# Layer B's normalized rows transposed by DMA instead of on TensorE

## The chip, the cores and the metric

One Trainium2 chip, one core. The metric is the device time of one execution of the whole program in microseconds, as the median of several runs. The time before is 1449.24 us (three runs, 1447.66 to 1451.28).

## The reference

Four layers, A B A B, on x of 2048 rows by 512 (f32). Both kinds use 32 heads of 16. Layers 0 and 2 share the weights of A, layers 1 and 3 those of B.

```
x = x + A(layernorm(x));  x = x + B(layernorm(x));  x = x + A(layernorm(x));  x = x + B(layernorm(x))

layernorm(x) = (x - mean) / sqrt(var + 1e-5)            # over the 512 of a row
A: q, k, v = x @ wqkv;  each row attends to 8 rows: itself and those 2, 4, ... 14 before it;  softmax;  @ wo
B: q, k, v = x @ wqkv;  each row attends to the 256 rows up to itself;  softmax;  @ wo
```

## The kernel before

**Chunks.** Rows are worked in 8 chunks of 256 (C), each as two halves of 128 rows. `layer_a(l, c)` and `layer_b(l, c)` describe one layer of one chunk. The calls are issued for layers 0 and 1, chunk by chunk (A0, B0, A1, B1, ... A7, B7), then for layers 2 and 3 (A8, B8 ... A15, B15). Here "chunk n of B" is B0 to B15. Layer B of a chunk needs layer A's output of the same chunk, and the keys and values of the chunk before it.

**Matrix products in two f16 parts.** A projection takes its rows as a high part xh (f16) and a low part xl (what the rounding left, f16), and the weights likewise: three f16 matmuls stand for one in f32 (lines 1015 to 1017 for the transposed outputs, 1035 to 1038 for the others). TensorE contracts over partitions, so xh and xl are needed transposed: features on partitions, rows along the free axis.

**The norm** (`norm`, line 923) is shared by both layers. Per half: statistics on VectorE (936, 939), then scale and shift for both halves (942 on VectorE, 945 on GpSimd, 948 on VectorE). Then it goes one of two ways, by the condition at line 957:

- Layer A, except the first chunk of layer 0: ScalarE writes the normalized half xn in f32 (964) and copies it to f16, ht (974); the rest xn - ht is computed in place on GpSimd or VectorE (970); two DMA transposes issued by SyncE move ht to xh (976) and the rest to xl (977).
- Layer B, and that first chunk: ScalarE writes xn (986), TensorE transposes its four 128 x 128 blocks in f32 into a PSUM bank (990), ScalarE casts the bank to xh (995), VectorE subtracts to get xl (996).

xn and ht have two buffers each, shared by all chunks; xh and xl have two of each.

**After the norm.** `proj_t` (1000) computes a projection in 16 steps of three matmuls for each 256 x 512 result; each step reads the whole of xh and xl, both halves. Layer B does that for keys and queries; the results are split in two f16 parts again (1270, 1273), written to DRAM (1283, "puts") and read back into a stacked layout (1294). Values and the output projection use `proj_n` (1030), 8 steps for each half. In `layer_b` a score step is one small group of four matmuls: first for the row maxima (1336, 1339, with VectorE's 1358 and 1354 behind it), then again for the exponentials (1430, 1432, then ScalarE's 1436 and GpSimd's mask 1445). The maxima reach the second group by way of DRAM (1391, 1397). A value step is 16 matmuls (1462). `finish` (1049) splits the attention's output (1059, 1061), projects it and adds it to x (1069); the sum is y, stored to DRAM (1080).

**The order.** Nothing is issued where it is written. Each step is a task for one engine's queue, added by `plan.add`; `ORDER` (line 40), a table written out in the file, gives each task its place in the queue of its engine, one list for each chunk of each layer. A negative place also moves the task to the other engine that it names (`alt`): the rests (970, 1061, 1203), the products of layer A (1152), the sums (1247 to 1251), the scaling of B's output (1537) and the scaled row maxima (1378, 1380). An engine takes its queue strictly in order. Steps of several chunks are interleaved in it: while a chunk of B is normalized, TensorE works on score and value steps and on the output projection of the B chunks before it.

```
if layers[l] == "A" and (l, c) != (0, 0):
    plan.add("ACT", 0.71, xnorm, r=[xs[t][1], vrs], w=[vxn])
    plan.add("ACT", 0.48, lambda xn=xn, ht=ht: nc.scalar.copy(ht.t, xn.t), r=[vxn], w=[vht])
    plan.add("POOL", 1.12, rest, r=[vxn, vht], w=[vlt], mode="S", alt=("DVE", 0.6))
    plan.add("SP", 1.24, ... nc.sync.dma_start_transpose(xh.t[:, :, sl], ht.t), r=[vht], w=[vh], size=16)
    plan.add("SP", 1.24, ... nc.sync.dma_start_transpose(xl.t[:, :, sl], low()), r=[vlt], w=[vl], size=16)
```

Of the kernel before, what the change touches and what calls it, by code (L numbers as in the profile page):

```python
# [19 lines left out]
S = 2048  # L20
# [5 lines left out]
W = 8  # L26
# [14 lines left out]
    "S": [4, 9, 6, 3],  # L41
    "pA": [3, -7, 2, 0, 8, 19, 10, 26, 15, 6, 18, 8, 21, 5, 3, 6, 4, 12, 27, 16, 33, 19, 30, 10, 25, 9, 24, 13, -30,
        10, 13, 8, 12, 11, 11, 33, 64, 39, 74, 42, 22, 46, 25, 51, 45, 26, 57, 27, 52],
    "pB": [14, 18, 15, 31, 17, 21, 22, 30, 24, 29, 26, 32, 19, 28, 27, -59, 59, 112, 66, 131, 68, 41, 100, 44, 84,
        71, 42, 96, 45, 89, 49, 99, 39, 88, 70, 51, 101, 43, 87, 24, 38, 51, 1, 29, 30, 28, 31],
    "W": [43, 0, 38, 89, 22, 20, 11, 1, 37, 12, 31, 39, 17, 2, 3, 14, 25, 41, 40, 23, 8, 66, 28, 58, 5, 84, 42, 13,
        35, 6, 7, 30, 15, 82, 9, 34, 24, 4, 16, 103, 92, 32, 36, 18, 10, 44, 85, 101, 88, 192, 116, 115, 86, 187,
        196, 189, 139, 90, 195, 193, 197, 100, 194, 87, 91, 165, 134, 190, 432, 448, 3387, 3365, 3254, 3451, 3389,
        3367, 3421, 3393, 3369, 3376, 3460, 3426, 3455, 3454, 3435, 3424, 3445, 3534, 3540, 3531, 3471, 3441, 3542,
        3536, 3543, 3527, 3539, 3533, 3526, 3535, 3541, 3537, 3440, 3459, 3437, 3448, 3461, 3446, 3538, 3532],  # L50
    "A0": [1, 0, 0, 2, 1, 3, 4, 5, 5, 1, 21, 5, 14, 2, 29, 7, 20, 0, 2, 45, 46, 47, 48, 49, 50, 51, 52, 67, 68, 69,
        71, 75, 76, 79, 81, 14, 24, 53, 54, 55, 56, 57, 59, 60, 61, 62, 63, 65, 70, 72, 77, 78, 80, 17, 23, 95, 97,
        98, 99, 105, 110, 113, 120, 94, 96, 102, 107, 108, 109, 118, 124, 36, 37, 12, 14, 37, 36, 38, 35, 73, 41, 44,
        40, 43, 83, 47, 48, 49, 50, 93, 54, 55, 53, 56, 104, 33, 11, 60, 61, 34, 62, 63, 64, 35, 65, 129, 67, 15, 73,
        17, 130, 69, 16, 72, -75, 136, 75, 18, 79, -81, 141, 76, -79, 77, 20, 46, 19, 166, 167, 168, 169, 170, 171,
        173, 175, 25, 83, 54, 50, -83, 178, 179, 180, 181, 182, 183, 184, 185, 18, 86, 84],
    "B0": [85, 91, 90, 92, 93, 22, 94, 53, 198, 55, 97, 54, 199, 56, 98, 200, 202, 206, 210, 212, 213, 214, 215, 201,
        203, 204, 205, 207, 208, 209, 211, 63, 105, 62, 104, 33, 35, 37, 36, 34, 32, 46, 45, 49, 53, 216, 217, 219,
        220, 222, 224, 227, 228, 218, 221, 223, 225, 226, 229, 230, 231, 65, 108, 64, 107, 41, 43, 40, 39, 44, 42,
        47, 48, 50, 52, 233, 235, 236, 238, 239, 244, 247, 248, 66, 234, 237, 240, 242, 243, 245, 249, 250, 67, 257,  # L60
        129, 253, 118, 258, 128, 252, 119, 251, 117, 255, 123, 254, 120, 259, 127, 130, 70, 132, 55, 56, 267, 71,
        273, 74, 42, 296, 271, 73, 275, 75, 43, 298, 78, 264, 136, 276, 150, 270, 144, 278, 151, 268, 141, 265, 145,
        272, 146, 261, 140, 153, 77, 155, 64, 65, 311, 84, 309, 83, 45, 378, 343, 87, 342, 88, 46, 387, 98, 305, 166,
        304, 167, 260, 131, 279, 149, 314, 171, 302, 165, 287, 164, 297, 162, 172, -174, 174, 66, 67, 388, 99, 368,
        94, 50, 436, 364, 93, 385, 97, 51, 438, 111, 285, 156, 319, 175, 365, 184, 360, 182, 320, 177, 359, 183, 313,
        170, 321, 176, 186, -189, 190, 87, 92, 412, 103, 406, 100, 52, 421, 418, 106, 424, 107, 56, 431, 109, 98, 95,
        99, 100, 251, 102, 103, 269, 270, 124, 71, 486, 487, 488, 489, 490, 491, 493, 495, 108, 284, 112, 125, 72,
        492, 496, 498, 499, 500, 501, 502, 503, 109, 285, 120],
    "A1": [12, 4, 22, 27, 7, 9, 28, 8, 31, 15, 16, -35, 16, 21, 19, 20, 10, 20, 23, 13, 21, 106, 111, 119, 121, 126,
        133, 135, 137, 138, 142, 150, 151, 152, 154, 155, 159, 40, 48, 114, 117, 122, 123, 125, 127, 128, 132, 147,  # L70
        157, 158, 160, 161, 162, 163, 164, 38, 47, 144, 146, 148, 153, 156, 172, 174, 191, 140, 143, 145, 149, 176,
        177, 186, 188, 52, 60, 23, 31, 106, -26, 81, 95, 232, 111, 109, -28, 110, 241, 113, 115, 112, 114, 246, 116,
        -30, -29, -31, 256, 121, 122, 68, 124, 125, 126, 69, -34, 262, 137, 36, 133, 34, 263, 135, 35, 134, -139,
        266, 139, 37, 142, 39, 269, 143, 40, 147, -149, 72, 38, 274, 277, 280, 281, 282, 283, 284, 286, 59, 152, 91,
        76, 41, 288, 289, 290, 291, 292, 293, 294, 295, 60, 158, 83],
    "B1": [154, 157, 159, 160, 161, 44, 163, 79, 306, 81, 169, 80, 307, 82, 168, 315, 316, 317, 318, 322, 323, 324,
        325, 326, 327, 329, 330, 331, 332, 333, 335, 85, 178, 86, 179, 72, 68, 73, 71, 69, 70, 80, 85, 86, 88, 328,
        334, 336, 341, 345, 347, 348, 349, 337, 338, 340, 344, 351, 352, 353, 354, 89, 180, 90, 181, 78, 79, 74, 75,
        77, 76, 81, 82, 90, 94, 399, 401, 410, 414, 419, 422, 423, 425, 108, 429, 430, 433, 434, 440, 441, 442, 445,
        112, 420, 223, 226, 394, 203, 209, 402, 208, 210, 389, 201, 202, 384, 195, 196, 407, 214, 216, 417, 219, 221,  # L80
        427, 229, 230, 232, 110, 234, 96, 97, 459, 119, 460, 118, 65, 469, 451, 115, 452, 116, 68, 481, 457, 117,
        447, 113, 67, 482, 466, 122, 470, 123, 69, 483, 126, 428, 231, 236, 454, 252, 254, 444, 241, 243, 435, 235,
        238, 449, 247, 249, 450, 248, 250, 443, 242, 245, 453, 255, 257, 259, 121, 265, 104, 106, 514, 137, 515, 139,
        75, 542, 506, 135, 513, 140, 76, 543, 546, 145, 529, 142, 77, 585, 540, 143, 552, 147, 78, 593, 156, 473,
        267, 268, 505, 287, 289, 504, 286, 288, 485, 276, 281, 467, 261, 263, 464, 258, 260, 484, 278, 279, 472, 266,
        274, 290, 136, 293, 113, 117, 572, 150, 573, 151, 79, 604, 595, 158, 592, 155, 82, 614, 596, 157, 616, 162,
        86, 626, 606, 159, 612, 160, 85, 627, 168, 528, 296, 298, 547, 301, 302, 560, 305, 307, 583, 315, 317, 582,
        314, 316, 571, 310, 312, 541, 299, 300, 561, 306, 308, 318, 153, 323, 136, 138, 624, 165, 625, 166, 89, 652,
        635, 170, 630, 169, 90, 655, 637, 171, 650, 174, 93, 662, 649, 175, 654, 176, 95, 664, 179, 142, 141, 148,
        149, 373, 150, 151, -106, -108, 189, 106, 702, 703, 704, 705, 706, 707, 708, 709, 116, 401, 182, 191, 109,  # L90
        710, 712, 714, 715, 716, 717, 718, 719, 157, 407, 162],
    "A2": [7, 9, 11, 13, 17, 23, 26, 7, 32, 59, 61, -104, 63, 58, 57, 58, -103, 62, 61, 26, 32, 339, 346, 350, 355,
        356, 357, 361, 362, 367, 369, 371, 372, 373, 374, 379, 383, 92, 95, 299, 300, 301, 303, 308, 310, 312, 358,
        363, 366, 370, 375, 376, 380, 381, 382, 91, 96, 390, 391, 393, 398, 400, 405, 408, 409, 392, 396, 397, 403,
        411, 413, 415, 416, 101, 104, 48, 53, -48, 187, 189, 185, 377, 192, 191, 194, 193, 386, 199, 197, 200, 198,
        395, 205, 207, 204, 206, 404, 211, 213, 102, 217, 218, 220, 105, -55, 426, 228, 57, 233, 58, 437, 239, 60,
        237, 59, 446, 246, 64, 244, 61, 439, 240, 63, 253, -257, 114, 62, 455, 456, 458, 461, 462, 463, 465, 468, 57,
        262, 105, 120, 66, 471, 474, 475, 476, 477, 478, 479, 480, 101, 271, 107],
    "B2": [264, 272, 273, 275, 277, 73, 280, 127, 494, 129, 282, 128, 497, 130, 283, 508, 509, 510, 512, 516, 517,
        518, 519, 507, 511, 520, 521, 523, 524, 526, 527, 138, 295, 141, 297, 125, 122, 118, 119, 123, 124, 132, 133,  # L100
        140, 146, 525, 531, 534, 538, 544, 545, 548, 549, 522, 530, 532, 533, 535, 536, 537, 539, 146, 304, 144, 303,
        129, 130, 127, 131, 128, 126, 135, 134, 139, 144, 631, 632, 633, 634, 638, 639, 642, 643, 172, 644, 646, 647,
        648, 651, 653, 658, 659, 177, 640, 350, 352, 613, 335, 336, 617, 339, 340, 602, 329, 331, 603, 328, 330, 629,
# [1510 lines left out]
```

## Time and profile before

| what | value |
|---|---|
| median of three runs | 1449.24 us |
| the profiled execution | 1449.52 us |
| its span, first to last instruction | 1447.8 us |
| mean granted TensorE clock | 0.961 |
| DMA traffic | 130.45 MB, mean 90 GB/s |
| transposes on TensorE (L990) | 136 |
| DMA transposes (L976, L977) | 30 and 30 |

In the lines of the profile PE is TensorE, PEld its weight loads, DVE is VectorE, ACT ScalarE, POOL GpSimd, SP SyncE; SPq is SyncE's queue, where DMAs are issued. L990 is line 990. A row of a timeline has the start in us, the length in us, the engine, the line, the operation and how many of them, and in brackets the idle time before it with what ended that. A row of a group has the busy time in us, the mean in ns, then the idle time of the engine just before and what ended it. A row of waits has who waited for whom: us in total, how often, the longest.

### The profile page before, as it was taken

Reading aid. Unit: us, or ns where it says so; the run is one execution under the profiler, and the core shown is the slowest. Engines: PE = TensorE matmul, PEld = TensorE weight load, DVE = VectorE, ACT = ScalarE, POOL = GpSimd, SP = SyncE. Lnnn points to the kernel's source line nnn. Section 1 sums busy time; section 2 is a strip of 40 time slices with the busy share of each in tenths; the row PEclk is TensorE's granted clock in tenths of the full one; section 3 lists DMA queues with packets and bytes.
Section 4 is the critical chain, followed back from the end, with each engine's and each line's share of the span. In section 5 each row is a group of like instructions: output and inputs, shape, how many; then the busy total and the mean of one; then the engine's idle time right before and its main releaser. Section 6 shows DMA issues by size and latency. Waiting matters only on the chain.

```text
span 1447.8 us, 35225 instructions
## 1 busy us (share of the span) xinstructions
PE 1343.2 (93%) x13918; PEld 780.3 (54%) x13918; DVE 1166.8 (81%) x2263; ACT 732.8 (51%) x1049; POOL 687.1 (47%) x780
## 2 busy tenths in 40 slices
PE   9985989999899999999999898999989999999997
PEld 7651636546364564746556363644637465474654
DVE  6867697896979879797996969698696977969694
ACT  6621335554565455555554444455454545445564
POOL 2415264472835427273471717355382743727233
PEclk9995989999999999999999999999999999999999
DMA  7232233225242333423233343323423143233232
GB/s 241 66 79 75 74 78 112 72 82 125 48 125 77 84 89 88 108 63 112 59 83 111 73 119 76 121 61 86 112 60 117 49 110 87 72 105 76 67 102 61
DMA packets 135944, 130.45 MB, mean 90 GB/s; under 512 B 68449, under 2 KB 94561, under 8 KB 135777
## 3 DMA queue, kind: packets, MB, share of 16 engines
q1 hardware_dynamic: 135520, 127.93, 32.6%
q8 instruction: 109, 1.79, 0.5%
q14 instruction: 59, 0.48, 0.1%
q10 hardware_dynamic: 256, 0.26, 0.1%
HBM read 67.11 MB, written 43.48 MB: 76 GB/s over the span
## 4 chain that ended last, share of the span: by engine, by line
PE 48%; DVE 21%; POOL 7%; issue 7%; DMA 6%; SPq 5%; ACT 5%; DVEq 0%; POOLq 0%; ACTq 0%
PE banks L1015 8%; PE banks L1016 7%; PE banks L1017 7%; PE banks L1462 5%; DVE m L1354 4%; PE banks L1160 3%; PE banks L1430 3%; DVE banks L1358 3%; ACT p L1436 3%; DVE pw L1242 3%; PE banks L1037 3%; PE banks L1035 3%; PE banks L1336 2%; POOL pw L1249 2%; PE banks L1038 2%
## 5 line engine op out<-in xcount | busy, mean ns | idle before, releaser
L1436 ACT ACTIVATE p<-banks,sclB 128x768 f32<-128x768 f32 x480 | 418.2, 900 | 282.4 <-PE banks L1432 203.9
L1445 POOL TENSOR_SCALAR_AFFINE_SELECT p<-p 128x1024 f32<-128x1024 f32 x240 | 263.5, 1106 | 345.0 <-ACT p L1436 300.7
L1354 DVE TENSOR_REDUCE m<-banks 128x2 f32<-128x512 f32 x448 | 296.9, 683 | 3.6
L1358 DVE COPY_PREDICATED banks<-maskt,banks 128x256 f32<-128x256 int16 x448 | 179.4, 420 | 65.0 <-PE banks L1339 55.5
L1462 PE MATMUL banks<-p,v 128*32 128x128 f32 (+1 forms) x3840 | 196.2, 332 | 5.7 <-POOL p L1445 4.4
L1152 DVE TENSOR_TENSOR pr<-kv,q 128x512 f32<-128x512 f32 x231 | 156.6, 727 | 31.6 <-PE banks L1160 17.5
L1462 PEld LDWEIGHTS banks<-p,v 128*32 128x32 f32 x3840 | 106.4, 110 | 97.6 <-issue 36.1
L1430 PE MATMUL banks<-stk,stk 64*128 64x256 f16 x960 | 133.7, 283 | 24.0 <-DVE m L1354 7.9
L1242 DVE TENSOR_TENSOR pw<-banks,kv 128x1024 f32<-128x1024 f32 x128 | 152.7, 1212 | 3.7 <-PE banks L1229 2.2
L1339 PE MATMUL banks<-stk,stk 48*128 48x128 f16 (+1 forms) x1024 | 128.5, 252 | 18.0 <-DVE m L1350 9.2
L1249 POOL TENSOR_TENSOR pw<-pw 128x512 f32<-128x512 f32 x100 | 127.3, 1273 | 13.5 <-DVE pw L1242 11.4
L1336 PE MATMUL banks<-stk,stk 48*128 48x128 f16 (+1 forms) x896 | 112.7, 253 | 20.1 <-DVE m L1354 9.2
L1430 PEld LDWEIGHTS <-stk 64*128 64x128 f16 x960 | 55.2, 94 | 119.4 <-issue 111.7
L1273 DVE SCALAR_TENSOR_TENSOR el<-banks,eh 128x512 f16<-128x512 f32 x64 | 42.6, 685 | 89.8 <-DMA re<-eh 45.2
L1432 PE MATMUL banks<-stk,stk 64*128 64x128 f16 x960 | 107.6, 222 | 0.0
L1336 PEld LDWEIGHTS <-stk 48*128 48x128 f16 x896 | 51.2, 94 | 100.3 <-issue 90.0
L1250 POOL TENSOR_TENSOR pw<-pw 128x256 f32<-128x256 f32 x100 | 73.0, 730 | 7.8
L1015 PE MATMUL banks<-xh,wB1h 128*128 128x256 f16 x256 | 71.0, 277 | 1.6 <-ACT p L1436 0.7
L1016 PE MATMUL banks<-xl,wA0h 128*128 128x256 f16 x256 | 70.1, 274 | 2.3 <-DMA xl<-xn 2.3
L1339 PEld LDWEIGHTS <-stk 48*128 48x128 f16 x1024 | 53.1, 96 | 34.6 <-issue 29.1
L1015 PE MATMUL banks<-xh,wA0h 128*128 128x256 f16 x256 | 70.4, 275 | 1.4 <-DMA xh<-ht 1.0
L1160 PE MATMUL banks<-pr,sel 128*32 128x512 f32 x512 | 71.0, 609 | 0.5 <-DVE pr L1152 0.3
(197 smaller groups left out, 3052.6 us busy)
## 6 DMA issues: line engine op xcount, KB each, us to landing
stk<-re SPq DMA_DIRECT2D x256, 96.0 KB
re<-eh SPq DMA_DIRECT2D x128, 128.0 KB
re<-el SPq DMA_DIRECT2D x64, 128.0 KB
xm<-y SPq DMA_DIRECT2D x32, 256.0 KB
y<-xm SPq DMA_DIRECT2D x32, 256.0 KB
oc<-os SPq DMA_DIRECT2D x120, 64.0 KB
os<-scr SPq DMA_DIRECT2D x15, 512.0 KB
x<-in_A_x_dram SPq DMA_DIRECT2D x16, 256.0 KB
```

Of the source, the lines that this page charges most:

```text
L1015: nc.tensor.matmul(ps[mp].t[:, i], wh, xh, start=k == 0, stop=False)
L1016: nc.tensor.matmul(ps[mp].t[:, i], wh, xl, start=False, stop=False)
L1152: E.tensor_mul(pr.t, window(kv[1].t, m, 64 * tq, 64)[:, 0], qb)
L1242: nc.vector.tensor_mul(pw.t, pb.t.unsqueeze(1).broadcast_to([P, 2, W, 64]), v)
L1336: nc.tensor.matmul(ps.t[:, par, 0 : (2 - qb) * P], lhs, stk[hf, bef][r, col, qb * P :], start=True, stop=True)
L1339: nc.tensor.matmul(ps.t[:, par, (2 - qb) * P : 3 * P], lhs, stk[hf, now][r, col, : (1 + qb) * P], start=True, stop=True)
L1354: nc.vector.tensor_reduce(out=m.t[:, :, u, qb], in_=ps.t[:, :, 0 : 2 * P], op=ALU.max, axis=AX.X)
L1358: nc.vector.copy_predicated(t[:, :, 0:P], maskt[:, 0:P].bitcast(I16).unsqueeze(1).broadcast_to([P, 2, P]), t[:, :, 2 * P : 3 * P])
L1430: nc.tensor.matmul(o[:, two], k[:, jf * P : (jf + 1) * P], q, start=True, stop=True)
L1436: nc.scalar.activation(pt.t[:, :, 2 * i : 2 * i + 2].rearrange("p s m q -> p m s q"), ps.t[:, :, : 3 * P].rearrange("p m (s q) -> p m s q" ...
L1445: nc.gpsimd.affine_select(out=v, in_=v, pattern=[[0, 8], [-1 if b == 0 else 1, P]], compare_op=ALU.is_gt if b == 0 else ALU.is_ge, fill=0. ...
L1462: nc.tensor.matmul(o, v[:, jj, 17 * h : 17 * h + 32], rhs, start=z == 0 and (b == 0 or first), stop=z == 1 and b == 1, tile_position=(0, 3 ...
```

## The change

One condition in `norm` is different. Layer A's chunks are treated as before; all of layer B's chunks take the way by DMA, too, except the first chunk of layer 1.

```diff
         for t in range(2):
-            if layers[l] == "A" and (l, c) != (0, 0):
+            if c or l > 1:
                 xn = buf("pxn", [P, D], F32, "xn", f"xn{l}_{c}_{t}")
                 ht = buf("pxn", [P, D], F16, "ht", f"ht{l}_{c}_{t}")
```

So in 15 chunks of B the transposes on TensorE (990), the casts (995) and the subtractions (996) are gone, and copies (974), rests (970) and DMA transposes (976, 977) take their place: per half one copy, one rest and two DMA transposes. A chunk of B has two tasks more. `ORDER` is another table throughout, with places for the new tasks and other places for the old ones; it also names other engines for some of them:

| tasks on their second engine | before | after |
|---|---|---|
| B's rests (970) on VectorE | - | 5 of 30 |
| A's rests (970) on VectorE | 13 of 30 | 13 of 30 |
| products (1152) on GpSimd | 25 of 256 | 32 of 256 |
| rests of e (1203) on GpSimd | 8 of 16 | 7 of 16 |
| sums (1247) on VectorE | 28 of 128 | 28 of 128 |
| scaled maxima (1380) on VectorE | 20 of 64 | 16 of 64 |
| scaling of B's output (1537) on GpSimd | 13 of 30 | 19 of 30 |
| rests of B's output (1061) on VectorE | 7 of 32 | 3 of 32 |

840 rows, old and new, of the table ORDER are left out of this document.

## The prediction

> **What bounds the kernel now.** I read the page first: its span, the busy times and the chain that ended last.
>
> ```profile
> span 1447.8 us, 35225 instructions
> PE 1343.2 (93%) x13918; PEld 780.3 (54%) x13918; DVE 1166.8 (81%) x2263; ACT 732.8 (51%) x1049; POOL 687.1 (47%) x780
> ...
> PE 48%; DVE 21%; POOL 7%; issue 7%; DMA 6%; SPq 5%; ACT 5%; DVEq 0%; POOLq 0%; ACTq 0%
> ```
>
> The profiled execution took 1449.5 us (1.7 around the span), the median of the three runs is 1449.24: one number for my purpose, and the sum is made against 1449.5. PE is busy for 93% of the span and is almost half of the chain; DVE at 81% is next. A busy PE can still be one that waits behind pipelined ends, so I looked at single stages and at PE's waits.
>
> ```profile
> 486.00:570.00 84.00, 80.42 (x881) 46.63 (x879) 70.29 (x124) 42.49 (x60) 39.34 (x44) 0.98 0.32 86
> ```
>
> ```profile
> PE banks L990 <- ACT xn L986: 10.2, 10, 3.5
> PE banks L1336 <- DVE m L1354: 9.2, 19, 2.1
> ```
>
> The columns of the stretch are us, then PE, PEld, DVE, ACT and POOL busy with counts, clock, DMA share, GB/s. In this stretch of 84 us, about one A chunk and one B chunk, PE idles only 3.6 us at a granted clock of 0.98, while DVE leaves 14 us and POOL over 40. So in the middle of the kernel **time is PE's own work plus the few waits that PE's order can't cover**. The largest of these waits belongs to the operation that the change removes: the transposes of line 990 wait 10.2 us for xn.
>
> **The PE side of the change.** 15 of B's 16 chunks change, two halves each: 30 halves, 120 transposes of the 136 (the rest is chunk 0 of layers 0 and 1).
>
> ```profile
> L990 PE MATMUL banks<-idf,xn 128*128 128x128 f32 x136 | 22.2, 290 | 12.3 <-ACT xn L986 10.2 <-DVE m L1354 1.3 <-DVE m L1350 0.3
> ```
>
> ```profile
> 82.36 1.97 PE L990 MATMUL banks<-idf,xn 128*128 128x128 f32 x8 [3.50 <-ACT xn L986]
> ...
> 231.37 0.65 PE L990 MATMUL banks<-idf,xn 128*128 128x128 f32 x4 [0.41 <-ACT xn L986]
> 231.86 0.59 PE L1035 MATMUL banks<-wB3h,ol 128*128 128x512 f16 x2
> 232.29 0.60 PE L990 MATMUL banks<-idf,xn 128*128 128x128 f32 x4
> 232.73 0.38 PE L1037 MATMUL banks<-wB3h,oh 128*128 128x512 f16 x1
> ```
>
> From the first of four transposes to the next matmul pass 0.49 us (231.37 to 231.86) and 0.44 (232.29 to 232.73): 0.46 x 30 = **13.9 us of PE less**. The group's busy time would give more (22.2 x 120/136 = 19.6), but that counts ends which overlap the next matmul; I take the spacing. The group also shows 12.3 us of idle PE just before it; 3.5 of that is at 82.36, in the chunk that keeps its transposes, so **8.8 us of waits go too**. Together 22.7 us, 1.5 per changed chunk.
>
> **What is late instead: the DMA path.** B's chunk is the place where a norm has no lead: its rows are those that layer A has just finished. This is one such chunk as it runs now:
>
> ```profile
> 398.18 0.38 PE L1035 MATMUL banks<-wA3h,ol 128*128 128x512 f16 x1
> 398.49 1.51 PE L1462 MATMUL banks<-p,v 128*32 128x256 f32 x32
> ...
> 404.48 0.28 PE L1430 MATMUL banks<-stk,stk 64*128 64x256 f16 x2
> ...
> 404.92 0.39 PE L1037 MATMUL banks<-wB3h,oh 128*128 128x512 f16 x1
> ...
> 408.36 0.28 PE L1015 MATMUL banks<-xh,wB1h 128*128 128x256 f16 x1
> ```
>
> ```profile
> 398.60 0.75 DVE L1069 SCALAR_TENSOR_TENSOR y<-banks,sclA,y 128x512 f32<-128x512 f32 x1 [0.53 <-PE banks L1035]
> ...
> 401.92 0.15 DVE L948 SCALAR_TENSOR_TENSOR rs<-mv,rs 128x2 f32<-128x2 f32 x1
> ```
>
> ```profile
> 402.11 1.52 ACT L986 ACTIVATE xn<-y,rs 128x512 f32<-128x512 f32 x2 [1.75 <-DVE rs L948]
> ...
> 420.32 1.14 ACT L974 CAST ht<-xn 128x512 f16<-128x512 f32 x2
> ```
>
> A's last output matmul starts at 398.18, y is ready at 399.35, the scale at 402.07, both xn at 403.6, and B's first projection starts at 408.36. After the change the two halves need the f16 copy (L974, the pair 1.14 us), the rest on POOL or DVE, and four DMA issues on SP. What the issues cost is in layer A's rows (the rests are priced in the fence of the part after this one):
>
> ```profile
> 331.15 2.56 SPq L977 DMA_TRANSPOSE xl<-xn  x2
> ...
> 928.80 1.21 SPq L976 DMA_TRANSPOSE xh<-ht  x1
> ...
> 1009.16 1.25 SPq L977 DMA_TRANSPOSE xl<-xn  x1
> ...
> 1015.77 1.28 SPq L976 DMA_TRANSPOSE xh<-ht  x1
> ...
> 1276.10 1.26 SPq L977 DMA_TRANSPOSE xl<-xn  x1
> ```
>
> ```profile
> 336.92 0.28 PE L1016 MATMUL banks<-xl,wA0h 128*128 128x256 f16 x1 [1.23 <-DMA xl<-xn]
> ...
> 931.27 0.28 PE L1015 MATMUL banks<-xh,wA0h 128*128 128x256 f16 x1 [0.28 <-DMA xh<-ht]
> ...
> 1019.37 0.27 PE L1015 MATMUL banks<-xh,wA0h 128*128 128x256 f16 x1 [0.75 <-DMA xh<-ht]
> ...
> 1280.60 0.28 PE L1016 MATMUL banks<-xl,wA0h 128*128 128x256 f16 x1 [1.07 <-DMA xl<-xn]
> ```
>
> An issue holds SP for 1.25 us. The four rows of PE are the only matmuls that waited for such a transpose, so they date its landing: 4.5 us after its issue began (332.43, the second of the pair at 331.15, to 336.9), 2.5, 3.6 and 4.5. So a transpose lands 2.5 to 4.5 us after the start of its issue.
>
> ```profile
> L1354 DVE TENSOR_REDUCE m<-banks 128x2 f32<-128x512 f32 x448 | 296.9, 683 | 3.6
> L1358 DVE COPY_PREDICATED banks<-maskt,banks 128x256 f32<-128x256 int16 x448 | 179.4, 420 | 65.0 <-PE banks L1339 55.5
> ```
>
> I read the rest from the order lists in the diff. Over chunks 1 to 15, 46 DVE steps of other work stand between the last y and the scale, where 63 stood: 17 fewer, at the mean of these two rows (0.55 us) 0.6 us per chunk. The copies follow the xn at once, and only three other jobs of SP stand among the 60 issues. So for this chunk: scale at 401.4, copies done by 401.4 + 1.5 + 1.1 = 404.0, first issue about 402.8, fourth at 402.8 + 3 x 1.25 = 406.6 (a POOL rest, 1.16 us behind the copy, is ready by then), landed **409.1 to 411.1**. PE's list now has, over these 15 stretches between A's last output step and B's first projection, 104 more score steps, 8 more value steps, 4 more output steps and 7 fewer of A's projections in place of 30 transposes. At 0.2 us a score step (two in 404.48 to 404.92), 0.75 a value step (two at 398.49) and a third for the others this is 26 less 14, 0.8 us per chunk: the first projection is due at **409.2**. It reads all four, so it waits 0 to 1.9 us, 15 times: 0 to 28 us. Layer A's 15 transposed chunks lost 3.3 us in all (1.23, 0.28, 0.75, 1.07), but their rows come from DRAM and can be fetched early. Here the projection falls due just as the transposes land, so I take the middle, 0.9: **13.5 us of new waits**.
>
> **What moves off DVE and on to POOL, ACT and SP.**
>
> ```profile
> L996 DVE TENSOR_TENSOR xl<-banks,xh 128x512 f16<-128x512 f32 x34 | 22.8, 685 | 11.9 <-ACT xh L995 11.7
> L970 POOL TENSOR_TENSOR xn<-xn,ht 128x512 f16<-128x512 f32 x17 | 19.5, 1159 | 22.5 <-ACT ht L974 20.1 <-PE banks L1432 2.4
> L970 DVE TENSOR_TENSOR xn<-xn,ht 128x512 f16<-128x512 f32 x13 | 9.2, 724 | 1.4 <-ACT ht L974 1.4
> L1537 POOL TENSOR_TENSOR oc<-oc,os 128x512 f32<-128x512 f32 x13 | 16.5, 1271 | 2.0 <-issue 2.0
> L1537 DVE TENSOR_TENSOR oc<-oc,os 128x512 f32<-128x512 f32 x17 | 11.2, 688 | 2.7 <-issue 1.5 <-DMA os<-scr 1.1
> L1152 DVE TENSOR_TENSOR pr<-kv,q 128x512 f32<-128x512 f32 x231 | 156.6, 727 | 31.6 <-PE banks L1160 17.5 <-ACT q L1131 11.7 <-ACT kv L1133 2.0
> L1152 POOL TENSOR_TENSOR pr<-kv,q 128x512 f32<-128x512 f32 x25 | 31.3, 1266 | 78.1 <-PE banks L1160 47.5 <-ACT q L1131 15.4 <-ACT kv L1133 15.2
> ```
>
> DVE loses 30 x 0.685 (L996); counting the negative places in the new lists, 25 of B's 30 rests go to POOL and 5 to DVE, 7 more products of L1152 and 6 more of L1537 go to POOL, and 4 more rests of L1061 (about the price of L970). DVE: -20.6 + 3.6 - 5.1 - 4.1 - 2.9 = -29 us. POOL: 29.0 + 8.9 + 7.6 + 4.6 = +50, to 51% of the span. ACT's copy of a half replaces its cast from the banks, one for one. I cost all this at nothing: PE's work hides it, and DVE and POOL have 14 and 40 us to spare per chunk. Where that cover is gone, it shows in waits like that of L1336 for m, 9.2 us in all: DVE's relief may take half of them away, and POOL's load, which sits between ACT and the value steps, may add as much, so 5 us either way.
>
> SP issues 60 more transposes, 75 us, 5 per chunk. Behind B's four stand the next A chunk's four in most lists, then the row maxima (L1391, L1397) and B's puts (L1283). B's first put needs a finished projection, 16 steps of a third of a us, 5 us after 409, and by then (402.8 + 10 = 413) those issues are about over: I take nothing, below it nothing can be gained, and the bound above is one issue per chunk (1.25 x 15 = 19 us).
>
> **Sum:** 1449.5 - 13.9 - 8.8 + 13.5 = 1440.3, so **1440 us**; about 0.3%, 4.4 us, is what a measurement of this kernel can tell from no change.
>
> **Rivals.**
> 1. *The waits are hidden.* Landing in 2.5 us, or score steps that cover it: 1449.5 - 22.7 = 1427. For it: layer A's 3.3 us. Against: A's lead of a chunk.
> 2. *The wait takes the place of what was removed.* At 1.5 us per chunk the gain is gone: 1449. For it: the 4.5 us landings are within the rows, two of the four.
> 3. *Slower: the DMA queue becomes the path.* From 1.5 us of wait per chunk on, it costs. With the late landing (1.9) and one issue behind another SP job (1.25) it is 3.15 x 15 = 47, 1449.5 - 22.7 + 47 = 1474; at two thirds of that 1458. For it: every landing counts here, and SP takes 5 us per chunk more. Against: the lists keep the four together.
> 4. *The transposes follow one another.* If each of the 16 blocks of a chunk went singly through one transposer, B's projection would come later by its whole length: at 4.5 us an instruction without overlap, 18 us after 402.8, 11.6 late per chunk, 1449.5 - 22.7 + 174 = 1601. The run of four speaks against it: between 1009.16 and 1019.37, in 10.2 us, all four of a chunk of layer A were issued and landed.
>
> The Trainium skill, "VectorE: DVE Perf Modes", section "The three transpose paths", gives 390 ns for a 128 x 128 block on TensorE and 1309 ns by DMA; by that rule alone this change looks wrong. With four blocks to an instruction that is an estimated 5.2 us, 21 for four in a row, and the sum 1644. The trace does not agree: 4.5 us at most for one, and 10.2 for four with other DMAs among them.
>
> **Chances.** Forecast (1432 to 1445) 0.36; hidden (below 1432) 0.22; taken back (1445 to 1454) 0.18; slower by the queue (above 1454) 0.22; in series 0.02. Faster by over 0.3% (below 1445.1): 0.58; within: 0.18; slower: 0.24. The range of 8 in 10 goes from 1422 (1427 with DVE's 5 us) to 1462, which leaves out the queue's dearer half and the series; the forecast's own is 1432 to 1445.
>
> **What would show it.** Right: L990 has 16 transposes and no 10 us wait; L976 and L977 have 60 each, L970 42 on POOL and 18 on DVE; PE busy falls by 14 to 20 us, DVE by about 29; PE's waits for xh and xl at L1015 and L1016 come to some 13 us in B's chunks. Wrong: these waits above 23 us, landings later than 4.5 us, or waits of L1430 for md and of L1336 for re that grow: then SP's queue is the path. If the time falls by more than 22.7 us, something beyond the transposes paid, DVE's relief or the new order.

## The result, and the profile after

The changed kernel takes **1463.72 us** (median of four runs, 1461.61 to 1466.35), the kernel before 1448.45 (1446.03 to 1451.28) in the runs beside it: the ratio is 1.0106, with a 95% interval from 1.0089 to 1.0124. The forecast was 1440, faster by 0.6%; the kernel is slower by 1.1%, just beyond the upper end of the range. Lines of the changed file from the norm on are two higher than before: L990 is now L992, L1336 is L1338, L1430 is L1432.

The page of the changed kernel, the lines that answer to those shown first of the kernel before (its profiled execution took 1461.61 us):

```profile
span 1459.9 us, 35092 instructions
PE 1338.9 (92%) x13798; PEld 776.0 (53%) x13798; DVE 1155.6 (79%) x2218; ACT 736.5 (50%) x1053; POOL 735.2 (50%) x821
...
PE 46%; DVE 22%; issue 8%; DMA 8%; POOL 7%; ACT 4%; SPq 4%; DVEq 0%; POOLq 0%; ACTq 0%
```

120 matmuls fewer, as many as transposes were removed, and yet PE is busy for only 4.3 us less (1343.2 before), while the span is 12.1 us longer. So PE's idle time (the span less its busy time) grew from 104.6 us to 121.0. Two things have to be found: what took PE's saved time back, and what PE now waits for.

To leave the first chunk and the tail out, I took one window from A's last output matmul in chunk 1 to the same matmul in chunk 15 (columns: start and end, length, then PE, PEld, DVE, ACT and POOL busy, clock, DMA share, GB/s). Before:

```profile
148.49:1338.37 1189.88, 1123.69 (x11850) 647.05 (x11849) 982.20 (x1875) 609.30 (x873) 595.03 (x658) 0.97 0.33 89
```

and after:

```profile
145.31:1349.36 1204.05, 1119.54 (x11744) 644.17 (x11742) 971.91 (x1834) 613.98 (x880) 633.07 (x690) 0.97 0.37 93
```

The loss is in these 14 chunks, 14.2 us or 1.0 us per chunk, with PE busy for 4.2 us less in them and the same granted clock.

**What took the saved time back.** The groups of PE by line, the score steps before:

```profile
L1430 PE MATMUL banks<-stk,stk 64*128 64x256 f16 x960 | 133.7, 283 | 24.0 <-DVE m L1354 7.9 <-ACT p L1436 6.8 <-DVE pw L1242 5.2
L1339 PE MATMUL banks<-stk,stk 48*128 48x128 f16 (+1 forms) x1024 | 128.5, 252 | 18.0 <-DVE m L1350 9.2 <-DMA stk<-re 2.8 <-DVE pw L1242 2.6
L1336 PE MATMUL banks<-stk,stk 48*128 48x128 f16 (+1 forms) x896 | 112.7, 253 | 20.1 <-DVE m L1354 9.2 <-ACT p L1436 4.2 <-DVE pw L1242 3.2
L1432 PE MATMUL banks<-stk,stk 64*128 64x128 f16 x960 | 107.6, 222 | 0.0
```

and after, with the first projection of B and the transposes that are left:

```profile
L1432 PE MATMUL banks<-stk,stk 64*128 64x256 f16 x960 | 138.4, 283 | 33.7 <-DVE m L1356 15.2 <-ACT p L1438 10.0 <-DVE pw L1244 3.1
L1341 PE MATMUL banks<-stk,stk 48*128 48x128 f16 (+1 forms) x1024 | 134.3, 251 | 17.8 <-DVE m L1352 7.0 <-DMA stk<-re 6.8 <-ACT p L1438 1.8
L1338 PE MATMUL banks<-stk,stk 48*128 48x128 f16 (+1 forms) x896 | 114.6, 252 | 33.8 <-DVE m L1356 19.6 <-ACT p L1438 5.0 <-DMA stk<-re 4.1
L1434 PE MATMUL banks<-stk,stk 64*128 64x128 f16 x960 | 110.5, 222 | 0.0
L1017 PE MATMUL banks<-xh,wB1h 128*128 128x256 f16 x256 | 73.1, 286 | 4.7 <-DMA xh<-ht 3.9 <-ACT xh L997 0.7
L1018 PE MATMUL banks<-xl,wB1h 128*128 128x256 f16 x256 | 73.1, 286 | 2.0 <-DMA xl<-xn 1.6 <-DVE xl L998 0.4
L992 PE MATMUL banks<-idf,xn 128*128 128x128 f32 x16 | 3.2, 354 | 3.8 <-ACT xn L988 3.8
```

Read the four score lines' counts, busy times and means together. Counts and means are the same (283, 251, 252, 222 ns), but the busy times add up to 497.8 us after, 482.5 before: 15.3 us more. Busy time counts a moment once, however many matmuls of a group run in it, so with equal means a higher busy time says that these small matmuls lay side by side less. That is about as much as the transposes had taken. The waits in the last part of the rows grew at two of the lines: for the row maxima m by 10.4 us at L1338 and 7.3 at L1432 (at L1341 they fell by 2.2). The transposes' landing itself shows as 3.9 + 1.6 = 5.5 us ahead of B's first projection.

**One chunk**, the one that the prediction followed. ScalarE:

```profile
405.75 1.52 ACT L966 ACTIVATE xn<-y,rs 128x512 f32<-128x512 f32 x2 [2.83 <-DVE rs L950]
407.18 1.12 ACT L976 CAST ht<-xn 128x512 f16<-128x512 f32 x2
```

SyncE's queue:

```profile
407.82 1.25 SPq L978 DMA_TRANSPOSE xh<-ht  x1
409.12 2.56 SPq L979 DMA_TRANSPOSE xl<-xn  x2
411.78 1.21 SPq L978 DMA_TRANSPOSE xh<-ht  x1
```

TensorE:

```profile
401.33 0.38 PE L1037 MATMUL banks<-wA3h,ol 128*128 128x512 f16 x1
...
407.90 0.29 PE L1432 MATMUL banks<-stk,stk 64*128 64x256 f16 x2 [0.56 <-DVE m L1356]
...
413.05 0.28 PE L1338 MATMUL banks<-stk,stk 48*128 48x256 f16 x2 [0.50 <-DVE m L1356]
...
414.34 0.27 PE L1017 MATMUL banks<-xh,wB1h 128*128 128x256 f16 x1 [0.36 <-DMA xh<-ht]
```

A's last output matmul is at 401.33 here. From it to the norm's xn pass 4.4 us (3.9 before), from there to the first issue 2.1, to the fourth 4.0 more, and that one lands 2.6 us after its issue began. So B's first projection starts 13.0 us after A's last output, where it was 10.2. The forecast had the first issue 4.6 us after A's last output matmul and the fourth 8.4 (402.8 and 406.6 less 398.18); here they come after 6.5 and 10.4, and over chunks 1 to 15 after 6.6 and 10.9 on average. So the chain of the norm is about 2 us later than forecast.

Over chunks 1 to 15 the stretch from A's last output to B's first projection has grown from 11.1 to 14.1 us on average. The sums over these 15 stretches, before and after (us, then the busy times):

```profile
sum 166.90, PE 155.06 PEld 78.21 DVE 149.13 ACT 91.75 POOL 67.03; mean PE 10.34 PEld 5.21 DVE 9.94 ACT 6.12 POOL 4.47
sum 211.24, PE 180.40 PEld 83.09 DVE 194.64 ACT 137.95 POOL 128.04; mean PE 12.03 PEld 5.54 DVE 12.98 ACT 9.20 POOL 8.54
```

PE is busy in them for 25.3 us more, mostly with score and value steps that stood elsewhere before, and idle for 30.8 us instead of 11.8. Of these 19.0 us of new idle time only 3.9 end with the landing of a transpose; the two brackets above show another kind, where a score step waits half a us for VectorE to give a bank back. What PE does while the rows are under way is not as cheap as forecast.

### The profile page after: what moved, and what is told of

Same layout as the page of the kernel before. It is cut to its first block, busy times and chain, and to the rows that moved or that the text cites. A ratio compares the mean times of both kernels' runs of the same rounds, so it can differ in the third digit from the quotient of the medians.

```text
span 1459.9 us, 35092 instructions
## 1 busy us (share of the span) xinstructions
PE 1338.9 (92%) x13798; PEld 776.0 (53%) x13798; DVE 1155.6 (79%) x2218; ACT 736.5 (50%) x1053; POOL 735.2 (50%) x821
## 4 chain that ended last, share of the span: by engine, by line
PE 46%; DVE 22%; issue 8%; DMA 8%; POOL 7%; ACT 4%; SPq 4%; DVEq 0%; POOLq 0%; ACTq 0%
PE banks L1017 8%; PE banks L1018 8%; PE banks L1019 8%; PE banks L1464 5%; DVE m L1356 5%; DVE banks L1360 4%; PE banks L1162 3%; PE banks L1432 3%; DVE pw L1244 2%; ACT p L1438 2%; POOL pw L1251 2%; PE banks L1039 2%; PE banks L1037 2%; PE banks L1338 2%; PE banks L1040 2%
## 5 line engine op out<-in xcount | busy, mean ns | idle before, releaser
L1154 DVE TENSOR_TENSOR pr<-kv,q 128x512 f32<-128x512 f32 x224 | 152.8, 732 | 37.8 <-PE banks L1162 22.2
L1432 PE MATMUL banks<-stk,stk 64*128 64x256 f16 x960 | 138.4, 283 | 33.7 <-DVE m L1356 15.2
L1341 PE MATMUL banks<-stk,stk 48*128 48x128 f16 (+1 forms) x1024 | 134.3, 251 | 17.8 <-DVE m L1352 7.0
L1338 PE MATMUL banks<-stk,stk 48*128 48x128 f16 (+1 forms) x896 | 114.6, 252 | 33.8 <-DVE m L1356 19.6
L1432 PEld LDWEIGHTS <-stk 64*128 64x128 f16 x960 | 59.0, 95 | 124.6 <-issue 119.3
L1338 PEld LDWEIGHTS <-stk 48*128 48x128 f16 x896 | 53.7, 94 | 120.2 <-issue 108.8
L1272 ACT ACTIVATE eh<-banks 128x512 f16<-128x512 f32 x64 | 37.4, 597 | 119.0 <-PE banks L1019 72.7
L972 POOL TENSOR_TENSOR xn<-xn,ht 128x512 f16<-128x512 f32 x42 | 48.7, 1164 | 56.1 <-ACT ht L976 49.0
L1154 POOL TENSOR_TENSOR pr<-kv,q 128x512 f32<-128x512 f32 x32 | 41.9, 1324 | 69.0 <-PE banks L1162 46.6
L1018 PE MATMUL banks<-xl,wB1h 128*128 128x256 f16 x256 | 73.1, 286 | 2.0 <-DMA xl<-xn 1.6
```

What stands on the lines that cost most here:

```text
L1018: nc.tensor.matmul(ps[mp].t[:, i], wh, xl, start=False, stop=False)
L1154: E.tensor_mul(pr.t, window(kv[1].t, m, 64 * tq, 64)[:, 0], qb)
L1338: nc.tensor.matmul(ps.t[:, par, 0 : (2 - qb) * P], lhs, stk[hf, bef][r, col, qb * P :], start=True, stop=True)
L1432: nc.tensor.matmul(o[:, two], k[:, jf * P : (jf + 1) * P], q, start=True, stop=True)
```

## The experiments

Theory at the start: TensorE's relief is real, and the DMA path's lateness takes more than it gives. The rival: the lists, not the transposes, are what changed the time. Ratios are against the kernel before, run beside each group.

### The parts, in the written order

**old_order_no_transposes.** The relief alone: the kernel before, its 30 halves' transposes not issued.

```diff
+            if c or l > 1:
...
+                    nc.scalar.copy(xh.t[:, :, sl], idf.unsqueeze(1).broadcast_to([P, 4, P]))
...
+                    nc.vector.tensor_sub(xl.t[:, :, sl], idf.unsqueeze(1).broadcast_to([P, 4, P]), xh.t[:, :, sl])
...
+                plan.add("PE", 0.48, lambda: None, r=[vxn], w=[vpt], mode="F", act=0.213)
```

> The kernel before, its order untouched, with B's 120 transposes not issued; the cast and the subtraction of each half read a constant tile instead of the PSUM bank (so B's projections get constant rows). This is what taking the work off TensorE is worth with nothing put in its place. Theory L (the change fails because the DMA path makes B's projections late): the removal is worth what was forecast, 22.7 us, so 1422 to 1432. Rival E (TensorE is not the bound, the other engines refill the gap): 1443 to 1450, within 0.4% of the kernel before.

Measured: 1451.41 us, ratio 1.0028 (1.0009 to 1.0047), near rival E's 1443 to 1450 and far from the 1422 to 1432 of theory L. Taking the transposes away gains nothing. The casts and subtractions of the constant tile take as long as before (609 and 686 ns for 582 and 685), so the stand-ins don't hide a gain. The busy times of its page and three of PE's waits show where it went:

```profile
PE 1331.4 (92%) x13798; PEld 769.8 (53%) x13798; DVE 1165.8 (81%) x2263; ACT 731.2 (51%) x1049; POOL 687.3 (48%) x780
```

```profile
PE banks L1349 <- DVE m L1367: 11.0, 22, 2.1
PE banks L1352 <- DVE m L1363: 10.3, 11, 5.7
PE banks L1443 <- DVE m L1367: 9.5, 21, 1.4
```

PE is busy for 11.8 us less than before, and the wait of the transposes for xn is gone but for the 3.6 us of the chunk that keeps them, yet the span is only 2.9 us shorter in the profiled execution, the fastest of its ten: PE stands idle for 113.5 us instead of 104.6, and its waits for all releasers on VectorE add up to 66.2 us instead of 50.0.

**new_order_no_transposes, new_order_unread, new_order_later.** The changed kernel, first with no transpose of B issued (copy and rest write xh and xl), then with all issued but a finished weight tile read in their place, then with three small DMAs ahead of B's first transpose.

```diff
 new_order_no_transposes
+                if layers[l] == "B":
...
+                        nc.scalar.copy(xh.t[:, :, sl], xn.t.rearrange("p (k t) -> p k t", k=4))
...
+                    plan.add("SP", 1.24, lambda: None, r=[vht], w=[vh], size=16)
```

```diff
 new_order_unread
-                xh, xl = d["xh"].t[:, k], d["xl"].t[:, k]
+                xh, xl = (x[:, k] for x in rows_of(l, c))
...
+            return [wt["B", 3, z][:, :, 0:C] for z in "hl"]
```

```diff
 new_order_later
+                    if layers[l] == "B" and t == first_half(l, c):
+                        for i in range(3):
+                            nc.sync.dma_start(aside[l, c][i], wt["B", 3, "h"][:, 0])
+                    nc.sync.dma_start_transpose(xh.t[:, :, sl], ht.t)
```

> The changed kernel, its order untouched, with B's DMA transposes not issued: copy and rest write straight into xh and xl (so B's projections get rows that are not transposed), which are ready some 6 us earlier. Theory L: only the waits for xh and xl and what they push along go away, 6.4 us of direct waits, up to 15 with what follows: 1448 to 1458. Rival O (the new order itself is the slow part, the DMAs cost nothing): 1459 to 1464. Rival B (the DMA and SyncE load of the transposes slows the other transfers): more than 15 us gained, below 1448.

> The changed kernel with all its DMA transposes issued, but B's projections read a finished weight tile in place of xh and xl, so they wait for no transpose. Theory L: like new_order_no_transposes within 3 us. Rival B (load on SyncE and the DMA engines): stays near the changed kernel, 1458 to 1464, and new_order_no_transposes is at least 8 us faster than this one. Rival O: 1459 to 1464 in both.

> The changed kernel with three plain DMAs of a finished tile to DRAM put on SyncE ahead of B's first transpose in each of 15 chunks, some 1.4 us of issue, so that B's four transposes land about 1.4 us later. Theory L (every us of that path counts): 0.7 to 1.4 us per chunk, 1474 to 1485. Rival O and rival E (the path has slack on the chip): under 5 us more, 1464 to 1468. Rival B: about 5 us more for 45 further DMAs, 1466 to 1470.

Measured: 1458.81 us (1.0068, 1.0046 to 1.0090), 1458.07 (1.0061, 1.0043 to 1.0078) and 1485.01 (1.0242, 1.0218 to 1.0265). The first two are the same: issuing 60 transposes costs nothing by itself, neither on SP's queue nor as DMA traffic. Not waiting for them gains 5.6 us, about the 5.5 us of waits seen above. But then 10 us of loss are left although nothing waits for a transpose and TensorE has less to do. By the sizes set beforehand that lies between theory L (up to 1458) and rival O (from 1459): two thirds of the loss stay in the change's lists when nothing has to land, be it for the cover that these lists hold or for something else in them.

In the third run 1.4 us of issue more per chunk cost 21 us. That is as much as was added, but its trace doesn't show it as lateness alone: the fourth issue comes 1.2 us later on average, B's first projection 0.55 us (14.63 us after A's last output, for 14.08), which is 8 us in 15 chunks. The granted clock is lower as well: 0.952 over 1483.1 us leaves 71 us of clock withheld, 0.961 over 1459.9 us leaves 57, so some 14 us more. Later rows cost in these lists; that every us of lateness counts in full is not shown.

### Is it VectorE?

The waits for m suggest that VectorE paces the score steps. So its selections were taken out, from the kernel before, from old_order_no_transposes and from the changed kernel.

```diff
-                        plan.add("DVE", 0.34, pick, r=[vps, vmask], w=[vpk])
+                        plan.add("DVE", 0.34, lambda: None, r=[vps, vmask], w=[vpk])
```

> The kernel before without the 448 selections of L1358 (the band of the scores that is selected is not written, so the attention weights are others); VectorE loses 448 x 0.42 = 179 us, nothing else moves. Theory V (VectorE's two steps on each block of scores, 0.42 and 0.68 us, pace TensorE's score steps of 0.2 us, so that what TensorE is relieved of turns into waits for the row maxima): TensorE's waits for m, 31 us in the kernel before, mostly vanish, about 1420. Theory O (the written order and other engines' chains hold the time, whatever VectorE does): above 1438.

> The same without layer B's 30 halves of TensorE transposes (13.9 us) either: the casts read a constant tile, so B's rows are others. Without the selections removed, this was worth nothing (1.0028 of before). Theory V: with VectorE out of the way TensorE's relief counts, 11 to 20 us below old_order_light. Theory O: within 5 us of it.

> The changed kernel without the selections. Theory V: its 104 more score steps between A's last output step and B's first projection then cost TensorE's 0.2 us each, the waits for m (42 us in the changed kernel) mostly vanish, and what is left of the loss against the kernel before is the landing's lateness (5 us) less the transposes removed (13.9): 0 to 12 us below old_order_light. Theory O: still 10 us or more above old_order_light.

Measured: 1438.81 us (0.9937, 0.9918 to 0.9955), 1442.50 (0.9964, 0.9947 to 0.9981) and 1451.64 (1.0020, 1.0000 to 1.0039). Theory V falls as far as the selections go; VectorE's other step on each block, the maximum (L1354 before), stays in all three. Without the selections VectorE is busy for 131 us less (not 179, since the recorded times of neighbouring steps overlap), and the wait of L1336 for m nearly disappears:

```profile
PE 1329.2 (93%) x13918; PEld 775.0 (54%) x13918; DVE 1036.0 (72%) x1815; ACT 732.8 (51%) x1049; POOL 690.3 (48%) x780
```

```profile
PE banks L1462 <- POOL p L1445: 13.6, 21, 2.1
PE banks L1430 <- ACT p L1436: 12.6, 22, 1.3
...
PE banks L1336 <- DVE m L1354: 1.9, 2, 1.7
```

Yet the time falls by only 9 us, TensorE's relief is again worth nothing (3.7 us slower), and the changed order still loses 12.8 us. A wait for m names who came last; behind it, others are about as late: all of TensorE's waits for m fall from 31.7 us to 17.8, while the value steps' wait for GpSimd's mask (L1462) goes from 4.4 to 13.6 and that of L1430 for ScalarE's exponentials from 6.8 to 12.6.

### Does an order without slack work both ways?

**old_order_twice.** The opposite of the first experiment: each of B's halves is transposed twice.

```diff
-                for k in range(4):
+                for k in (*range(4), *range(4 if c or l > 1 else 0)):
```

> The kernel before with each of layer B's 30 halves of TensorE transposes issued twice, the second over the first (output unchanged): 13.9 us more TensorE work in the same order. Theory P (packed: the chains through TensorE, VectorE and ScalarE are about equally long, so that relief of one brings nothing and an addition to any of them costs in full): 10 to 14 us slower, ratio 1.007 to 1.010. Theory Q (TensorE has slack at this place, its work here is free): within 4 us, ratio up to 1.003.

Measured: 1461.10 us, ratio 1.0075 (1.0047 to 1.0104). Adding 13.9 us costs 11; removing 13.9 gains nothing. That is what theory P says: the lists are packed so that the chains through several engines are about equally long. By that theory PE is on the longest, so an addition counts, and a removal only leaves the next chain in its place. The run doesn't single PE's work out, though: the second transposes also delay B's own rows, whose first projection starts 11.7 us after A's last output instead of 11.1. What the relief is worth can be seen only with lists that were made for it.

### Lists searched again

For the next runs the order lists were searched anew by local search over the places and the second engines, with the durations of the planner (the model in the file that lays the tasks out in time), a transpose landing 1 us later than its 0.9. Beside that, searched_no_transposes has the edit of old_order_no_transposes, searched_dma_unread that of new_order_unread, and searched_no_landing and grown_no_landing that of new_order_no_transposes. What such a kernel leaves out has no duration in its planner; searched_dma_unread has the lists of searched_dma. The two grown kernels start farther from their goal and, which no run shows, were searched for longer, both alike, with every task free to go back to its first engine.

```diff
-                landed = dma + 0.9
+                landed = dma + 0.9 + (1.0 if t.us == 1.24 else 0.0)
```

> The kernel before with other order lists: a local search over them, and in the planner a DMA transpose lands 1 us later than its 0.9 us (as the traces show for layer A). Theory P: some 0 to 8 us faster than before. It is the yardstick for the two runs that follow, whose lists were searched in the same way and as long.

> As searched_tensor, but without layer B's 30 halves of TensorE transposes (the casts read a constant tile, so B's rows are others), the lists searched for that. In the written order their absence was worth nothing. Theory P: once the order is refitted a part of the 13.9 us shows, 5 to 14 us below searched_tensor. Theory Q: within 4 us of it.

> The changed kernel with lists searched in the same way and as long, a DMA transpose landing 1 us later in the planner. Theory L (the longer way of B's rows through copy, issue and landing is what costs, order or not): 8 us or more above searched_tensor. Theory W (only the lists of the change were unlucky, fitted to a landing that is too early): within 4 us of searched_tensor or below it.

> As searched_dma (1482.81 us), all copies and transposes issued, but layer B's projections read a finished weight tile in their place (so B's results are others) and wait for no landing. Theory L1 (what costs is the order that has to be built round a later landing, not the waits left in it, as in the written order of the change, where this took away 5.6 of 15 us): down by 0 to 10 us, above 1472. Theory L2 (the landings still come late and that is the loss): down by 20 us or more, below 1463.

> The changed kernel with copies and rests on the engines that the change gives them, but the copy and the rest write xh and xl directly, no transpose is issued (so B's rows are not transposed and its results are others), and the lists are searched, in the same way and as long as searched_dma's, for rows that are ready when copy and rest are done. Theory M (the time from the first issue to the last landing, 7 to 8 us a chunk for which the lists must find cover, is what costs): near searched_no_transposes (1442.97), below 1455. Theory N (the copies and the rests, moved to GpSimd, are what costs): within 10 us of searched_dma (1482.81), above 1470.

> The kernel before with a second draw of searched lists: how far do lists that were searched alike differ? searched_tensor took 1459.29 us. If draws differ by 5 us or less, the distances of 16 and 23.5 us between searched_no_transposes, searched_tensor and searched_dma stand; if by 15 or more, those distances say little.

> searched_no_landing (1471.01 us) again, its search started from the lists of the kernel before instead of those of the change (what it leaves out is the same: no transpose is issued, B's rows are not transposed). Theory N (copies and rests on their engines cost, whatever the lists started from): again above 1465. Theory S (the change's lists carry something slow that the planner does not see, and searches that start from them inherit it): near searched_no_transposes (1442.97), below 1455.

> The changed kernel, complete, with lists searched from those of the kernel before. Theory L (the longer way of B's rows costs, from whatever lists one starts): above 1470. Theory S (searches from the change's lists inherit what is slow in them): below 1460.

| run | what carries B's rows | lists searched from those of | us | ratio (95%) |
|---|---|---|---|---|
| searched_tensor | TensorE, as before | before | 1459.29 | 1.0066 (1.0044 to 1.0088) |
| searched_tensor_2 | the same, a second draw | before | 1457.50 | 1.0056 (1.0041 to 1.0071) |
| searched_no_transposes | nothing | before | 1442.97 | 0.9952 (0.9933 to 0.9970) |
| grown_no_landing | copy and rest, nothing lands | before | 1440.99 | 0.9942 (0.9914 to 0.9971) |
| grown_dma | DMA, as in the change | before | 1475.95 | 1.0173 (1.0136 to 1.0209) |
| searched_dma | DMA, as in the change | the change | 1482.81 | 1.0224 (1.0200 to 1.0247) |
| searched_dma_unread | all issued, not waited for | the change | 1478.53 | 1.0208 (1.0161 to 1.0254) |
| searched_no_landing | copy and rest, nothing lands | the change | 1471.01 | 1.0151 (1.0129 to 1.0172) |

The expectation that searched_tensor would gain was a miss: a search by the planner's durations loses 9 to 10 us against the written lists of before, and grown_dma is 12 us slower than the change with its own lists. So searched lists are compared with one another; two draws from the same start differ by 1.8 us, while other starts differ by far more (point 2).

1. **The relief is worth 16.5 us between lists that were searched for each** (1.0066 less 0.9952, 0.0114 of 1448). It shows as PE's busy time, 1333.3 us instead of 1348.1, with the same idle time (107.8 for 107.6). Against the written lists of before the same kernel gains 7 us (0.0048 of 1448). Theory Q falls.
2. **Copies and rests cost nothing that shows.** searched_no_landing, 28 us above searched_no_transposes, spoke for theory N. Searched from the lists of before, with 16 of B's rests on GpSimd instead of 22, the same work takes 1441 us. Theory N falls; what it showed is that lists grown from the change's carry a loss of their own (30 us here, from 1440.99 to 1471.01), which the search did not remove. The clock has a part in it: 0.951 was granted over 1471.1 us, 0.963 over 1438.6 in grown_no_landing, some 19 us more withheld.
3. **The landing costs 33.5 us between the two grown kernels** (1.0173 less 0.9942): by their edits, issue and landing are all that grown_dma has and grown_no_landing lacks. Taking the change with its own lists, the fastest on record with a landing, it is 24 us (1.0106 less 0.9942). Theory L holds. Theory W falls as far as this search goes; that better lists for the DMA path exist is not ruled out.
4. Not waiting (searched_dma_unread) gives back 4.3 us, within its interval. As in the written order, most of the price isn't in the waits for the transposes.

Where the 33.5 us are, in the window from A's last output matmul of chunk 1 to that of chunk 15. grown_no_landing:

```profile
146.97:1327.68 1180.71, 1110.93 (x11743) 636.48 (x11742) 975.13 (x1843) 605.20 (x872) 628.40 (x689) 0.97 0.33 89
```

grown_dma:

```profile
140.41:1362.89 1222.48, 1131.62 (x11738) 638.26 (x11737) 980.97 (x1841) 609.37 (x873) 630.26 (x691) 0.96 0.35 92
```

With the same work, 41.8 us more (it had run 6.6 us ahead at the start of the window): PE is busy for 20.7 us more and idle for 21.1 more. PE's waits for the row maxima in the two runs, grown_no_landing first, and the only one of grown_dma for a transpose:

```profile
PE banks L1439 <- DVE m L1363: 13.9, 31, 1.2
...
PE banks L1345 <- DVE m L1363: 9.7, 17, 1.8
```

```profile
PE banks L1328 <- DVE m L1346: 16.5, 28, 2.6
PE banks L1422 <- DVE m L1346: 14.9, 28, 2.1
...
PE banks L1008 <- DMA xl<-xn: 0.5, 1, 0.5
```

Half a us is all that waits for a transpose. The stretch from A's last output to B's first projection is 14.2 us per chunk, against 10.7 in grown_no_landing; the lists fill it with steps that they take from elsewhere. The score lines are busy for 496.1 us instead of 486.9, with means within 2 ns, which is less than half of the 20.7; the clock column has more of it, 0.96 for 0.97, and over the whole runs (0.958 over 1474.6 us, 0.963 over 1438.6) some 9 us more of clock were withheld. That the moved steps are what costs, there and here, is the reading that fits these numbers; no run isolates it.

No version with the whole computation beat the kernel before.

## Why the prediction was wrong

- **What bounds the kernel.** "Time is PE's own work plus the few waits that PE's order can't cover" held in one direction only. 13.9 us more PE work cost 11, 13.9 less gained nothing in that order. A share of 93% and the transposes on the chain of waits didn't tell how close the second longest chain is.
- **The PE side, 22.7 us.** The count was right: L992 keeps 16 transposes. So was the wait: the idle time just ahead of them went from 12.3 us to 3.8, 8.5 less where 8.8 were forecast. What failed is that it would show in the time. By the runs the relief is worth nothing in the order of before, 7 us against it in an order made for it, and 16.5 us between searched orders; in this change 4.3 us of it show in PE's busy time, because the score lines lost 15.3 us.
- **The DMA path, the step that failed.** The single costs were about right: issues of 1.25 us, and landings of 2.5 to 4.7 us after the issue in the six chunks where B's first projection waited for one, for a forecast of 2.5 to 4.5. The start was wrong: the first issue was put 4.6 us after A's last output and came after 6.6 on average. The scale was read from one chunk in which it is early (xn starts 3.9 us after A's last output there, 5.4 on average over chunks 1 to 15 before, 4.9 after), and both xn run ahead of the first copy. So the due time was wrong, too: "26 less 14, 0.8 us per chunk" of cover, where the stretch grew by 3.0. That much cover made the direct waits small, 5.5 us for the 13.5 of the sum. But the sum took cover as free, and it isn't: the 15 stretches grew by 44 us, of which 25 are PE busy, where the forecast's steps come to 12, and 19 PE idle, only 3.9 of it for a landing. A part of this comes back elsewhere, and 14.2 us are lost in the window. By the searched lists the landing with its cover was worth 33.5 us, by the fastest lists on record 24, where 13.5 stood in the sum. 33.5 less the relief of 16.5 is a loss of 17, and measured was 15.3 (1463.72 less 1448.45); that the two come so near is in part luck, since the searched lists are 8 to 12 us slower than the written ones on both sides.
- **VectorE, GpSimd, SyncE.** GpSimd came out as forecast (48.1 us more for 50), 42 rests on it and 18 on VectorE. VectorE fell by 11.2, not 29. Costing them at nothing held as far as it was tried: with no transposes issued the time is the same as with all issued and unread (1458.81 and 1458.07), and with copies and rests in place of casts and subtractions grown_no_landing is no slower than searched_no_transposes (1440.99 and 1442.97). The products and scalings moved to GpSimd were not tried by themselves.
- **The rivals.** Rival 3 had the size (1458 to 1474), but not the mechanism: SP's queue is not the path, and the waits for xh and xl are far below the 23 us that it named as its sign. Its other sign, growing waits for re, did appear (L1338 and L1341 together 10.9 us for 4.5), but most of it is there without any issue, too (6.1 and 2.6 in new_order_no_transposes), so it belongs to the order. One landing of 4.65 us is just beyond the 4.5 that it named. Rivals 1, 2 and 4 fell. By the Trainium skill's rule from "VectorE: DVE Perf Modes", section "The three transpose paths", the DMA path is the dearer one for a block, and the measured sign agrees. The 1644 us estimated from its figures don't: here the four transposes of a chunk are issued and landed within 6.6 us (407.82 to 414.34), and most of that is covered.

**What stays open.** Why the score matmuls lie side by side less is seen, not explained. It is so in the lists of the change, in those grown from them even where nothing lands (501.7 us in searched_no_landing), and in grown_dma. It is the same without VectorE's selections (488.5 us in new_order_light, 472.4 in old_order_light), so these are not the reason. Nor is it shown what the change's lists carry that the lists grown from those of before don't, or how near to the best any of these lists are.

## What to carry to other kernels

In a kernel whose order is packed by hand or by a search, test a relief by itself before counting it: leave the work out in the order as it is, and add the same amount. If adding costs and removing doesn't, several chains may be tied, and the relief is worth something only in an order made for it. Price a longer latency by what has to be moved to cover it, not by the wait that is left at its end: here the wait was 5.5 us and the price 24 to 33.5. And read a lead from all chunks, not from one: here the one that was read lay 1.5 us ahead of the average.

## What the runs showed of the hardware

A late projection also ran slower in one run. In new_order_later, B's first projection after a wait of 1.73 us, then its group:

```profile
421.27 0.27 PE L1032 MATMUL banks<-xh,wB1h 128*128 128x256 f16 x1 [1.73 <-DMA xh<-ht]
421.38 0.30 PE L1033 MATMUL banks<-xl,wB1h 128*128 128x256 f16 x1
421.48 0.41 PE L1034 MATMUL banks<-xh,wB1l 128*128 128x256 f16 x1
421.69 0.42 PE L1032 MATMUL banks<-xh,wB1h 128*128 128x256 f16 x1
```

```profile
L1032 PE MATMUL banks<-xh,wB1h 128*128 128x256 f16 x256 | 76.2, 298 | 7.4 <-DMA xh<-ht 4.2 <-ACT xn L974 2.4 <-ACT xh L1012 0.7
```

The spacing goes from 0.11 to 0.21 us; the mean is 298 ns where it was 277 before and 286 after the change, and the clock of the whole run is 0.952 for 0.961. Here the wait is followed by a stretch at about half the clock. The wait isn't shown to be its cause, since in the changed kernel the clock falls at the same place with no long wait. Windows of 2 us around the projection at 414.34 (the clock is the number after the five engines):

```profile
411.00:413.00 2.00, 1.31 (x20) 0.67 (x17) 2.00 (x5) 1.75 (x3) 0.72 (x1) 1.00 0.39 75
413.00:415.00 2.00, 1.50 (x19) 1.03 (x19) 1.92 (x5) 2.00 (x4) 1.59 (x3) 1.00 0.76 230
415.00:417.00 2.00, 2.00 (x11) 1.17 (x8) 1.65 (x4) 1.37 (x3) 1.03 (x1) 0.51 0.56 128
417.00:419.00 2.00, 2.00 (x15) 1.35 (x15) 1.44 (x4) 0.00 (x0) 0.12 (x1) 0.64 0.97 305
```

PE is busy for 2.8 of the 4 us ahead, on small score matmuls, and no wait there is longer than half a us; then 2 x 0.49 + 2 x 0.36 = 1.7 us of clock are lost in the next 4 us, as much as 3.4 us at half the clock. The Trainium skill, "TensorE: Matmul & The Clock Gate", Part 1, names a window of about 3.4 us, which agrees, and lets the clock fall after an idle window; here 4 us that were 70% busy came ahead of it. Over the whole run such losses are equal before and after the change (0.961 both), so they don't explain the result; they are part of what new_order_later, searched_no_landing and grown_dma lost.
